# Swapping weights and stream in the output matmuls of a chunked linear attention ahead of two expert layers

## The chip, the cores and the metric

The kernel runs on one core of a Trainium2 chip. The metric is the device time of one launch, in microseconds. Two per cent of it is 22 us.

## The reference

A gated linear attention feeds a top-2 mixture of experts, and that a dense two-layer network. There are 4 batches, 8 heads, 768 steps, head dimension 48; so 3072 tokens of 384 features.

```python
for t in range(S):
    state = alpha[:, :, t, :, None] * state + k[:, :, t, :, None] * v[:, :, t, None, :]
    y[:, :, t] = einsum('bhd,bhde->bhe', q[:, :, t], state)
x = y as tokens x (heads * 48)
noisy = x @ w_gate + log1p(exp(x @ w_noise)) * noise      # 8 experts
top 2 of noisy, softmax of the two -> weights
x = sum over the two experts of weight * (relu(x @ w1[e]) @ w2[e])   # F = 1024
h = x @ w_in                                               # 2048
return max(0.01 * h, h) @ w_out
```

## The kernel before

**Attention** works on 24 units: a unit is 128 consecutive tokens of one batch, all eight heads, two heads of a pair side by side on the partitions (rows 0 to 47 and 64 to 111). Four units make a tile (six tiles), six units a batch. Per unit, by the names of the code: SyncE loads `at` (decays), `kq` (keys and queries), `nv` (values, tokens on rows); VectorE scans the decays (`back`, `forth`) and scales keys and queries (`keys` L918, `queries` L922); TensorE transposes the keys (`turn_k` L930), makes the scores of each head (`score` L943, 48 rows of one half of the array for each head of a pair), ScalarE copies them out of the accumulator, GpSimd masks them in two halves (`mask_s` L952, tile `am`). The state goes on through `update` L975 and `carry` L979, GpSimd decays it (`sp`, L968).

The output of a unit collects in the accumulator tile `pY`, tokens on rows. `within` (L996) adds masked scores times values: the weights are 128 columns of `am`, the stream 48 columns of `nv`, four matmuls for the even heads and four for the odd ones in two steps. `across` (L1001) adds queries times decayed state: the weights are the queries `qp` of a pair, the stream 96 columns of `sp`; the first unit of a batch has none. `copy_y` (L1017) copies `pY` into the tile's `x`, and SyncE stores it to `x_d` in DRAM (L1022).

**Routing** per tile: `turn_x` (L1040) transposes the four units' `x` in twelve pieces, `copy_x` (L1045) copies them, `logits` (L1050) multiplies them by the gate weights in three matmuls of 512 columns, `turn_back` (L1059) brings tokens back on rows; VectorE picks the top two, and GpSimd scatters token numbers into slots by indirect DMA (L1148).

**Experts** (`gemm1` L668, `gemm2` L707) run on rows gathered from `x_d` (L510, transposed at L528), weights split in two parts for three matmuls each; the dense network follows with the same lines. The first two experts' groups need the routing and the stores of the first four tiles only; their slot numbers come in by one DMA (`load_idx` L505).

All instructions are put in order by a list scheduler, `Planner`: each step has an engine, a duration, what it depends on, buffer rings that it takes, and a due time; `plan.run(1, core)` writes out the attention stage, `plan.run(2)` the rest. Every engine, SyncE's queue of DMAs too, then runs its list strictly in that order. Matmuls are plain fp32 in attention and routing; each leaves two records in the profile.

A second function, `general`, holds a slower way for inputs outside certain bounds; it stands in a branch that these inputs don't take.

Of the kernel before, what the change touches and what calls it, by code (L numbers as in the profile page):

```python
# [323 lines left out]
def tile_kernel(  # L324
# [16 lines left out]
    wgn_l: bass.AP,  # L341
    noise_l: bass.AP,
# [53 lines left out]
    wgn = consts.tile([128, KD, 2 * E], FT)  # L396
# [433 lines left out]
    with ExitStack() as actx:  # L830
# [13 lines left out]
            at=5, kq=4, nv=5, suf=3, wt=3, kt=4, qp=4, pM=2, kN=2, pS=1, pT=1, ar=2, am=2, sp=2, S=2, pY=1, x=2, xt=1,  # L844
# [7 lines left out]
        def build_unit(u):  # L852
# [118 lines left out]
            if not last:  # L971
                def update():
                    d["pu"] = psum.tile([PP, HP, P2], FT, name="pM", bufs=2)
                    for p in range(HP):
                        nc.tensor.matmul(d["pu"][:, p, :], d["kN"][:, p, :], d["v"][:, p * P2:(p + 1) * P2],  # L975
                                         start=p == 0, stop=first, skip_group_check=True)
# [9 lines left out]
                up = add("p", 0.72, update, use=[(ck, R["kN"]), (LV, R["nv"])], takes=[R["pM"]], due=b + 3.2)  # L986
# [16 lines left out]

            w0 = add("p", 0.92, lambda: within(0), use=[(sel[0], R["am"]), (LV, R["nv"])], takes=[R["pY"]],
                     due=b + PERIOD + 3)
            w1_ = add("p", 0.92, lambda: within(1), [w0, sel[1]], use=[(sel[0], R["am"]), (LV, R["nv"]), (w0, R["pY"])],
                      due=b + PERIOD + 4)
            done = w1_
            if not first:
                done = add("p", 0.92, across, [w1_], use=[(qq, R["qp"]), (dc, R["sp"]), (w0, R["pY"])],  # L1010
                           due=b + PERIOD + 5)
# [7 lines left out]
            cy = add("a", 0.5, copy_y, [done] + xs[T], use=[(w0, R["pY"])] + ([(xs[T][0], R["x"])] if c else []),  # L1019
                     takes=[] if c else [R["x"]])  # L1020
            xs[T].append(cy)
            xo = add("s", 0.07, lambda: nc.sync.dma_start(x_d[u * C:(u + 1) * C, :], X[T][:, c, :]), [cy],  # L1022
                     use=[(xs[T][0], R["x"])], size=0.2)
# [7 lines left out]
        def build_turn(T, gr, keep):  # L1031
# [3 lines left out]
            def turn_x(d):  # L1035
                if d == 0 and T == gr[0]:
                    keep["lg"] = rt.tile([128, NG * len(gr), 2 * E], FT, name="lg")
                k["px", d] = ps2.tile([128, TT], FT, name="pA")
# [3 lines left out]
            def copy_x(d):  # L1042
                if d == 0:
                    k["xt"] = early.tile([128, KD, TT], FT, name="xt", bufs=1)
                nc.scalar.activation(k["xt"][:, d, :], k["px", d], AF.Copy)  # L1045

            def logits():
                k["pl"] = ps2.tile([2 * E, TT], FT, name="pA")
                for d in range(KD):
                    nc.tensor.matmul(k["pl"], wgn[:, d, :], k["xt"][:, d, :], start=(d == 0), stop=(d == KD - 1))  # L1050

            def copy_l():
                k["lt"] = k["xt"][:2 * E, 0, :]
                nc.scalar.activation(k["lt"], k["pl"], AF.Copy)

            def turn_back():
                k["pb"] = ps2.tile([128, NG, 2 * E], FT, name="pA")
                for c in range(NG):
                    nc.tensor.transpose(k["pb"][:, c, :], k["lt"][:, c * C:(c + 1) * C], identf[:2 * E, :2 * E])  # L1059

            def copy_back():
                nc.scalar.activation(keep["lg"][:, n0:n0 + NG, :], k["pb"], AF.Copy)

            b = at_unit(4 * T + 5)
            cp = []
            before = done_of.get(("chain", RGROUPS.index(gr) - 2), [])[-1:]
            for d in range(KD):
                tx = add("p", 0.46, lambda d=d: turn_x(d), xs[T] + before, use=[(xs[T][0], R["x"])], takes=[R["pA"]],
                         due=b + 2 + 2 * d)
                core.append(tx)  # L1070
                cp.append(add("a", 0.61, lambda d=d: copy_x(d), use=[(tx, R["pA"])] + ([(cp[0], R["xt"])] if d else []),
                              takes=[] if d else [R["xt"]]))
# [361 lines left out]
```

## Time and profile before

| | us |
|---|---|
| median of 3 runs | 1101.55 |
| lowest and highest run | 1100.0, 1129.27 |
| profiled execution, its own time | 1096.46 |
| span of its trace | 1094.7 |

The span runs from the first to the last instruction of the profiled execution; 1.8 us of its own time lie around it. The median of the runs is 5.1 us above the profiled execution's time. Attention and routing take about the first 195 us of the span, the experts and the dense network the rest.

### The profile page before, as it was taken

Reading aid. Unit: us, or ns where it says so; the run is one execution under the profiler, and the core shown is the slowest. Engines: PE = TensorE matmul, PEld = TensorE weight load, DVE = VectorE, ACT = ScalarE, POOL = GpSimd, SP = SyncE. Lnnn points to the kernel's source line nnn. Section 1 sums busy time; section 2 is a strip of 40 time slices with the busy share of each in tenths; the row PEclk is TensorE's granted clock in tenths of the full one; section 3 lists DMA queues with packets and bytes.
Section 4 is the critical chain, followed back from the end, with each engine's and each line's share of the span. In section 5 each row is a group of like instructions: output and inputs, shape, how many; then the busy total and the mean of one; then the engine's idle time right before and its main releaser. Section 6 shows DMA issues by size and latency. Waiting matters only on the chain.

```text
span 1094.7 us, 17345 instructions
## 1 busy us (share of the span) xinstructions
PE 1068.6 (98%) x6404; PEld 1017.5 (93%) x6404; DVE 586.8 (54%) x1199; ACT 389.1 (36%) x829; POOL 324.6 (30%) x386
## 2 busy tenths in 40 slices
PE   7999998999999999999999999999999999999997
PEld 6877886899999999999999999999999999999997
DVE  8588974522445554754565334554555555454543
ACT  3665553322344453533453333231222212121211
POOL 3457766531113333444253131320111102010000
PEclk9999896999999999999999999999999999999999
DMA  9868832233345364655566555320101111100000
GB/s 245 239 180 194 176 82 86 39 92 107 121 124 184 125 208 148 209 168 154 172 206 226 198 190 181 115 66 7 59 12 55 29 37 30 37 23 22 1 23 25
DMA packets 76965, 125.76 MB, mean 115 GB/s; under 512 B 10407, under 2 KB 57383, under 8 KB 76871
## 3 DMA queue, kind: packets, MB, share of 16 engines
q1 hardware_dynamic: 68679, 104.47, 31.9%
q0 software_dynamic: 8192, 20.09, 6.5%
q8 instruction: 52, 0.85, 0.3%
q14 instruction: 42, 0.34, 0.1%
HBM read 91.84 MB, written 32.69 MB: 114 GB/s over the span
## 4 chain that ended last, share of the span: by engine, by line
PE 93%; POOL 2%; issue 2%; DVE 1%; ACT 1%; DMA 1%; POOLq 0%; ACTq 0%; DVEq 0%
PE py L707 40%; PE ph L668 39%; PE pY L996 3%; PE pA L528 2%; PE pS L943 2%; PE pY L1001 2%; PE pM L975 1%; PE pA L1050 1%; PE pM L979 1%; DMA at<-in_al_l_dram 1%; PE pM L930 1%; PE pA L1040 1%; POOL am L952 1%; POOL idx_d L1148 1%; DVE kt L918 0%
## 5 line engine op out<-in xcount | busy, mean ns | idle before, releaser
L692 DVE SCALAR_TENSOR_TENSOR hl<-ph,hh 128x384 fp32r<-128x384 f32 (+1 forms) x128 | 77.6, 606 | 202.7 <-ACT hh L685 186.6
L678 ACT ACTIVATE hc<-ph 128x384 f32<-128x384 f32 x128 | 62.9, 492 | 294.9 <-PE ph L668 289.6
L681 DVE SCALAR_TENSOR_TENSOR hc<-hc 128x384 f32<-128x384 f32 x128 | 71.5, 558 | 174.6 <-ACT hc L678 173.0
L685 ACT ACTIVATE hh<-ph 128x384 fp32r<-128x384 f32 (+1 forms) x128 | 68.0, 531 | 261.3 <-PE ph L668 247.8
L707 PE MATMUL py<-w2hA,hh 128*128 128x384 f32 (+1 forms) x416 | 142.1, 342 | 0.0
L707 PE MATMUL py<-w2hB,hh 128*128 128x384 f32 (+1 forms) x416 | 141.7, 341 | 0.0
L707 PE MATMUL py<-w2hA,hl 128*128 128x384 f32 (+1 forms) x416 | 140.5, 338 | 0.0
L707 PE MATMUL py<-w2lA,hh 128*128 128x384 f32 (+1 forms) x416 | 140.2, 337 | 0.0
L707 PE MATMUL py<-w2lB,hh 128*128 128x384 f32 (+1 forms) x416 | 140.0, 337 | 0.0
L707 PE MATMUL py<-w2hB,hl 128*128 128x384 f32 (+1 forms) x416 | 140.0, 337 | 0.0
L668 PE MATMUL ph<-xh,w1hA 128*128 128x384 f32 (+1 forms) x384 | 136.0, 354 | 0.9 <-issue 0.9
L668 PE MATMUL ph<-xl,w1hA 128*128 128x384 f32 (+1 forms) x384 | 134.2, 350 | 0.2 <-issue 0.2
L668 PE MATMUL ph<-xh,w1hB 128*128 128x384 f32 (+1 forms) x384 | 133.9, 349 | 0.0
L668 PE MATMUL ph<-xh,w1lA 128*128 128x384 f32 (+1 forms) x384 | 133.9, 349 | 0.0
L668 PE MATMUL ph<-xl,w1hB 128*128 128x384 f32 (+1 forms) x384 | 133.6, 348 | 0.0
L668 PE MATMUL ph<-xh,w1lB 128*128 128x384 f32 (+1 forms) x384 | 133.5, 348 | 0.0
L730 POOL DMA_INDIRECT xg<-y_d,gidx x48 | 48.7, 1015 | 263.2 <-PE pA L528 212.5
L510 POOL DMA_INDIRECT xg<-x_d,idx x56 | 55.7, 994 | 106.4 <-PE pA L528 87.0
L707 PEld LDWEIGHTS py<-w2hA,hh 128*128 128x128 f32 (+1 forms) x416 | 77.3, 186 | 1.2 <-issue 0.3
L707 PEld LDWEIGHTS py<-w2lA,hh 128*128 128x128 f32 (+1 forms) x416 | 77.3, 186 | 0.9
L707 PEld LDWEIGHTS py<-w2lB,hh 128*128 128x128 f32 (+1 forms) x416 | 77.3, 186 | 1.0
L707 PEld LDWEIGHTS py<-w2hB,hh 128*128 128x128 f32 (+1 forms) x416 | 77.3, 186 | 0.8
(153 smaller groups left out, 1989.0 us busy)
## 6 DMA issues: line engine op xcount, KB each, us to landing
w1s<-in_moe_w_dram SPq DMA_DIRECT2D x32, 384.0 KB
w2s<-in_moe_w_dram SPq DMA_DIRECT2D x32, 384.0 KB
kq<-in_kq_l_dram SPq DMA_DIRECT2D x24, 448.0 KB
w1s<-in_moe_w_in_dram SPq DMA_DIRECT2D x24, 256.0 KB
w2s<-in_moe_w_out_dram SPq DMA_DIRECT2D x16, 384.0 KB
y_d<-ys SPq DMA_DIRECT2D x32, 180.0 KB
at<-in_al_l_dram SPq DMA_DIRECT2D x24, 226.2 KB
nv<-in_v_l_dram SPq DMA_DIRECT2D x24, 192.0 KB
```

What stands on the lines that cost most here:

```text
L510: nc.gpsimd.indirect_dma_start(out=xg[:n, :], out_offset=None, in_=x_d[0:rows, :], in_offset=bass.IndirectOffsetOnAxis(ap=idx_sb[i][:n, j, ...
L528: nc.tensor.transpose(p[:, d, :n], src[:n, d * 128:(d + 1) * 128], identf[:n, :n])
L668: nc.tensor.matmul(ps[:, :n], a[:, d, fo:fo + 128], x[:, d, :n], start=i == 0, stop=i == len(seq) - 1)
L678: nc.scalar.activation(hc[:, :n], ps[:, :n], AF.Copy)
L681: nc.vector.scalar_tensor_tensor(hc[:, :n], hc[:, :n], 0.01, hc[:, :n], op0=OP.mult, op1=OP.max)
L685: nc.scalar.activation(hh[:, :n], ps[:, :n], AF.Relu)
L692: nc.vector.scalar_tensor_tensor(hl[:, :n], ps[:, :n], 0.0, hh[:, :n].bitcast(FT), op0=OP.max, op1=OP.subtract)
L707: nc.tensor.matmul(py[:n, :], h[:, o:o + n], w[:, f % 2, :], start=(f == 0 and i == 0), stop=(f == nf - 1 and i == 2))
L730: nc.gpsimd.indirect_dma_start(out=yg, out_offset=None, in_=y_d[0:rows, :], in_offset=bass.IndirectOffsetOnAxis(ap=gidx[:, c, kk:kk + 1], ...
L943: nc.tensor.matmul(d["pa", i][:, p], d["kt"][r, p], d["qp"][r, p], start=True, stop=True)
L996: nc.tensor.matmul(d["py"][:, p, i * D:(i + 1) * D], d["am"][:, i, p, :], d["v"][:, h * D:(h + 1) * D], start=h == 0, stop=first, skip_gro ...
L1001: nc.tensor.matmul(d["py"][:, p, :], d["qp"][:, p], d["sp"][:, p].rearrange("p s d -> p (s d)"), start=False, stop=True, skip_group_check= ...
```

## The change

`within` now uses 64 columns of values as weights (48 and 16 zeros) and streams the 128 columns of masked scores; the even head of a pair writes rows 0 to 63 of `pY`, the odd one rows 64 to 127. `across` uses 48 columns of the state as weights and streams the queries, into the same halves. So `pY` has features on rows, tokens on columns. It is copied as it is into the tile's `xt`; `logits` reads it from there, in four matmuls for the four head pairs, with gate weights that are laid out the same way with zeros between (`wgp_l`). For the store to `x_d`, each unit's output is transposed by four matmuls (`turn_y`) and copied once more (`copy_x`). The values are padded on the host to 64 columns a head, and `update` reads its 96 columns in two pieces of 48. `turn_x` and its copies are gone. `within` is one step that needs both halves of the mask. Due times and durations in the planner follow. Line numbers after the diff are 1 higher from L339 on, and differ by a few more behind L996.

```diff
-    wgn = consts.tile([128, KD, 2 * E], FT)
+    wgn = consts.tile([128, HP, 2 * E], FT)
...
-            at=5, kq=4, nv=5, suf=3, wt=3, kt=4, qp=4, pM=2, kN=2, pS=1, pT=1, ar=2, am=2, sp=2, S=2, pY=1, x=2, xt=1,
+            at=5, kq=4, nv=5, suf=3, wt=3, kt=4, qp=4, pM=2, kN=2, pS=1, pT=1, ar=2, am=2, sp=2, S=2, pY=1, x=3, xt=2, lt=1,
...
-                d["v"] = loads.tile([128, Dm], FT, name="nv", bufs=5)
-                nc.sync.dma_start(d["v"], v_l[u * C:(u + 1) * C, :])
+                d["v"] = loads.tile([128, H, 64], FT, name="nv", bufs=5)
+                nc.sync.dma_start(d["v"].rearrange("p h d -> p (h d)"), v_l[u * C:(u + 1) * C, :])
...
-                        nc.tensor.matmul(d["pu"][:, p, :], d["kN"][:, p, :], d["v"][:, p * P2:(p + 1) * P2],
+                        nc.tensor.matmul(d["pu"][:, p, :], d["kN"][:, p, :], d["v"][:, 2 * p:2 * p + 2, 0:D],
...
-            def within(i):
-                if i == 0:
-                    d["py"] = psum.tile([128, HP, P2], FT, name="pY", bufs=1)
+            def within():
+
+                d["py"] = psum.tile([128, HP, C], FT, name="pY", bufs=1)
                 for p in range(HP):
-                    h = 2 * p + i
-                    nc.tensor.matmul(d["py"][:, p, i * D:(i + 1) * D], d["am"][:, i, p, :], d["v"][:, h * D:(h + 1) * D],
-                                     start=h == 0, stop=first, skip_group_check=True)
+                    for i in range(2):
+                        nc.tensor.matmul(d["py"][64 * i:64 * i + 64, p], d["v"][:, 2 * p + i, :], d["am"][:, i, p, :],
+                                         start=p == 0, stop=first, skip_group_check=True)
...
-                    nc.tensor.matmul(d["py"][:, p, :], d["qp"][:, p], d["sp"][:, p].rearrange("p s d -> p (s d)"),
-                                     start=False, stop=True, skip_group_check=True)
...
+                    for i in range(2):
+                        nc.tensor.matmul(d["py"][64 * i:64 * i + D, p], d["sp"][:, p, i, :], d["qp"][:, p],
+                                         start=False, stop=True, skip_group_check=True)
+
+            w0 = add("p", 1.0, within, use=[(s_, R["am"]) for s_ in sel[:1]] + [(LV, R["nv"])], deps=sel, takes=[R["pY"]],
+                     due=b + PERIOD + 4)
...
-                    X[T] = work.tile([128, NG, Dm], FT, name="x")
-                nc.scalar.activation(X[T][:, c, :], d["py"].rearrange("p h d -> p (h d)"), AF.Copy)
...
+                    X[T] = work.tile([128, NG, HP, C], FT, name="xt")
+                nc.scalar.activation(X[T][:, c], d["py"], AF.Copy)
+
+            def turn_y():
+                d["px"] = ps2.tile([128, HP, C], FT, name="pA")
+                for p in range(HP):
+                    nc.tensor.transpose(d["px"][:, p, :], X[T][:, c, p, :], identf)
+
+            def copy_x():
+                d["x"] = work.tile([128, HP, 2, D], FT, name="x", bufs=3)
+                nc.scalar.activation(d["x"], d["px"].rearrange("p h (s d) -> p h s d", s=2)[:, :, :, 0:D], AF.Copy)
...
+            ty = add("p", 0.46, turn_y, [cy], use=[(xs[T][0], R["xt"])], takes=[R["pA"]], due=b + PERIOD + 8)
+            cx = add("a", 0.5, copy_x, use=[(ty, R["pA"])], takes=[R["x"]])
+            xo = add("s", 0.07, lambda: nc.sync.dma_start(x_d[u * C:(u + 1) * C, :], d["x"].rearrange("p h s d -> p (h s d)")),
+                     use=[(cx, R["x"])], size=0.2)
...
-                for c in range(NG):
-                    nc.tensor.transpose(k["px", d][:, c * C:(c + 1) * C], X[T][:, c, d * 128:(d + 1) * 128], identf)
...
-                nc.scalar.activation(k["xt"][:, d, :], k["px", d], AF.Copy)
...
-                k["pl"] = ps2.tile([2 * E, TT], FT, name="pA")
-                for d in range(KD):
-                    nc.tensor.matmul(k["pl"], wgn[:, d, :], k["xt"][:, d, :], start=(d == 0), stop=(d == KD - 1))
...
+                k["pl"] = ps2.tile([2 * E, NG, C], FT, name="pA")
+                for p in range(HP):
+                    nc.tensor.matmul(k["pl"], wgn[:, p, :], X[T][:, :, p, :], start=(p == 0), stop=(p == HP - 1))
```

How the instructions of TensorE move, first around the logits of the first tile. `pA` is the accumulator of transposes and logits, `xg` the gathered rows, `ph` and `py` the experts' accumulators. Before:

```order
L943 MATMUL pS<-qp,kt 128x128 x8
L979 MATMUL pM<-sp,identf 112x384
L1040 MATMUL pA<-identf,x 128x128 x8
L996 MATMUL pY<-nv,am 128x48 x4
L1040 MATMUL pA<-identf,x 128x128 x4
L996 MATMUL pY<-nv,am 128x48 x4
L943 MATMUL pS<-qp,kt 128x128 x8
L1050 MATMUL pA<-xt,wgn 16x512 x3
L1001 MATMUL pY<-sp,qp 128x96 x4
L930 MATMUL pM<-identf,kt 128x112 x4
L1059 MATMUL pA<-identf,xt 128x16 x4
```

With the change:

```order
L997 MATMUL pY<-am,nv 64x128 x8
L1022 MATMUL pA<-identf,xt 128x128 x4
L1003 MATMUL pY<-qp,sp 48x128 x8
L944 MATMUL pS<-qp,kt 128x128 x8
L980 MATMUL pM<-sp,identf 112x384
L1050 MATMUL pA<-xt,wgn 16x512 x4
L1022 MATMUL pA<-identf,xt 128x128 x4
L931 MATMUL pM<-identf,kt 128x112 x4
L944 MATMUL pS<-qp,kt 128x128 x8
L1059 MATMUL pA<-identf,lt 128x16 x4
```

The twelve transposes of a tile (x8 and x4) ahead of the logits are gone; transposes x4 of single units stand between the other groups, one of them behind the logits; `within` is x8 in one place and has 64-column weights, `across` is x8.

The end of the attention stage on TensorE, up to the first transposes of gathered rows. Before:

```order
L1001 MATMUL pY<-sp,qp 128x96 x4
L1119 LDWEIGHTS tri
L1119 MATMUL pA<-ot,tri 128x32
L1120 LDWEIGHTS ones_b
L1120 MATMUL pA<-acc,ones_b 128x32
L996 MATMUL pY<-nv,am 128x48 x8
L1001 MATMUL pY<-sp,qp 128x96 x4
L1040 MATMUL pA<-identf,x 128x128 x12
L528 MATMUL pA<-identf,xg 128x128 x3
L1050 MATMUL pA<-xt,wgn 16x512 x3
L528 MATMUL pA<-identf,xg 128x128 x3
L1059 MATMUL pA<-identf,xt 128x16 x4
```

With the change:

```order
L1022 MATMUL pA<-identf,xt 128x128 x8
L997 MATMUL pY<-am,nv 64x128 x8
L1022 MATMUL pA<-identf,xt 128x128 x4
L1003 MATMUL pY<-qp,sp 48x128 x8
L1050 MATMUL pA<-xt,wgn 16x512 x4
L1113 LDWEIGHTS tri
L1113 MATMUL pA<-ot,tri 128x32
L1114 LDWEIGHTS ones_b
L1114 MATMUL pA<-acc,ones_b 128x32
L1022 MATMUL pA<-identf,xt 128x128 x4
L1059 MATMUL pA<-identf,lt 128x16 x4
L529 MATMUL pA<-identf,xg 128x128 x12
```

The last logits stand ahead of the position matmuls (`tri`) of the tile before, the transposes of gathered rows behind all of attention and not between its last groups.

SyncE's queue at the same place, `x_d<-x` being the stores of the output and `idx` the slot numbers of the first experts. Before:

```order
L1022 DMA x_d<-x 128x384
L870 DMA nv<-in_v_l_dram 128x384
L1022 DMA x_d<-x 128x384
L866 DMA kq<-in_kq_l_dram 112x1024
L1022 DMA x_d<-x 128x384 x4
L505 DMA idx_119<-idx_d 128x24
L1022 DMA x_d<-x 128x384
```

With the change:

```order
L1033 DMA x_d<-x 128x384
L871 DMA nv<-in_v_l_dram 128x512
L867 DMA kq<-in_kq_l_dram 112x1024
L1033 DMA x_d<-x 128x384 x9
L506 DMA idx_119<-idx_d 128x24
L1033 DMA x_d<-x 128x384
L444 DMA w1s<-in_moe_w_dram 128x3x256 x2
L447 DMA w2s<-in_moe_w_dram 128x2x384 x2
```

The slot numbers are loaded behind 23 of the 24 stores in both; nine stores stand together ahead of them where there were four.

## Rows read from the trace of the kernel before

**Rows 1.** Page, part 1: busy time, share of the span, instructions.
```profile
PE 1068.6 (98%) x6404; PEld 1017.5 (93%) x6404; DVE 586.8 (54%) x1199; ACT 389.1 (36%) x829; POOL 324.6 (30%) x386
```

**Rows 2.** Page, part 4: the chain that ended last, by line.
```profile
PE py L707 40%; PE ph L668 39%; PE pY L996 3%; PE pA L528 2%; PE pS L943 2%; PE pY L1001 2%; PE pM L975 1%; PE pA L1050 1%; PE pM L979 1%; DMA at<-in_al_l_dram 1%; PE pM L930 1%; PE pA L1040 1%; POOL am L952 1%; POOL idx_d L1148 1%; DVE kt L918 0%
```

**Rows 3.** Stretches: length, busy us (x instructions) of each engine, granted clock, DMA share, GB/s.
```profile
23.20:112.00 88.80, 84.64 (x750) 71.08 (x751) 69.19 (x155) 52.81 (x124) 53.30 (x79) 1.00 0.81 212
112.00:118.70 6.70, 6.70 (x38) 5.81 (x35) 6.36 (x15) 3.74 (x10) 5.40 (x8) 0.50 0.63 126
118.70:170.00 51.30, 48.75 (x412) 39.45 (x411) 41.98 (x105) 27.28 (x66) 35.09 (x52) 1.00 0.48 109
170.00:187.00 17.00, 15.53 (x77) 14.02 (x77) 3.58 (x19) 5.16 (x11) 8.12 (x9) 0.50 0.23 67
...
193.80:197.30 3.50, 3.28 (x10) 2.80 (x11) 3.36 (x11) 1.98 (x4) 2.63 (x3) 0.51 0.69 58
197.30:1091.00 893.70, 889.53 (x5026) 869.10 (x5024) 437.30 (x859) 283.58 (x587) 205.98 (x201) 1.00 0.33 103
```

**Rows 4.** Waits of TensorE, 0 to 165 us: total us, times, longest.
```profile
PE pY L996 <- POOL am L952: 2.7, 4, 1.2
```

**Rows 5.** Timeline, 11 to 181 us: start us, us, engine, line, tiles, count [idle before <-releaser].
```profile
11.81 1.94 PE L996 MATMUL pY<-nv,am 128*128 128x48 f32 x8 [0.23 <-POOL am L952]
...
168.21 2.05 DVE L918 TENSOR_TENSOR kt<-kq,suf 112x512 f32<-112x512 f32 x1
...
170.31 1.01 PE L930 MATMUL pM<-identf,kt 112*128 112x112 f32 x4 [1.64 <-DVE kt L918]
...
177.51 3.62 PE L996 MATMUL pY<-nv,am 128*128 128x48 f32 x16 [0.57 <-POOL am L952]
```

**Rows 6.** Timeline, 87 to 90 us: one within group, loads and matmuls.
```profile
87.78 1.86 PEld L996 LDWEIGHTS pY<-nv,am 128*128 128x128 f32 x16 [1.69 <-POOL am L952]
...
87.80 1.96 PE L996 MATMUL pY<-nv,am 128*128 128x48 f32 x16 [1.09 <-POOL am L952]
```

**Rows 7.** Timeline of TensorE, 34 to 40 us.
```profile
34.27 1.00 PE L996 MATMUL pY<-nv,am 128*128 128x48 f32 x8
35.20 1.16 PE L943 MATMUL pS<-qp,kt 48*128 48x128 f32 x16
36.29 1.09 PE L996 MATMUL pY<-nv,am 128*128 128x48 f32 x8
37.22 0.99 PE L975 MATMUL pM<-nv,kN 128*112 128x96 f32 x8
38.05 1.06 PE L1001 MATMUL pY<-sp,qp 112*128 112x96 f32 x8
39.03 1.16 PE L943 MATMUL pS<-qp,kt 48*128 48x128 f32 x16
```

**Rows 8.** Timeline of TensorE, 62 to 71 us: transposes and logits.
```profile
62.92 1.09 PE L1040 MATMUL pA<-identf,x 128*128 128x128 f32 x8
63.85 0.94 PE L975 MATMUL pM<-nv,kN 128*112 128x96 f32 x8
...
65.28 0.60 PE L1040 MATMUL pA<-identf,x 128*128 128x128 f32 x4
65.72 0.99 PE L996 MATMUL pY<-nv,am 128*128 128x48 f32 x8
...
67.73 2.75 PE L1050 MATMUL pA<-xt,wgn 128*16 128x512 f32 x6
70.41 1.09 PE L996 MATMUL pY<-nv,am 128*128 128x48 f32 x8
```

**Rows 9.** Groups by line, ScalarE, 23 to 168 us: the copies.
```profile
L1017 ACT ACTIVATE x<-pY 128x384 f32<-128x384 f32 x21 | 10.3, 489 | 14.4 <-PE pY L1001 9.2 <-issue 1.4 <-PE pY L996 1.4
...
L1045 ACT ACTIVATE xt<-pA 128x512 f32<-128x512 f32 x15 | 8.8, 598 | 0.9 <-PE pA L1040 0.7
```

**Rows 10.** Page, part 6: loads of the values, KB each.
```profile
nv<-in_v_l_dram SPq DMA_DIRECT2D x24, 192.0 KB
```

More of the change, by code (lines that the diff above doesn't have):

```diff
@@ L341, in tile_kernel @@
     wgn_l: bass.AP,
+    wgp_l: bass.AP,
     noise_l: bass.AP,
@@ L984, in step @@
                     nc.scalar.activation(d["S"], d["pu"].rearrange("p h (s d) -> p h s d", s=2), AF.Copy)
-                up = add("p", 0.72, update, use=[(ck, R["kN"]), (LV, R["nv"])], takes=[R["pM"]], due=b + 3.2)
+                up = add("p", 0.9, update, use=[(ck, R["kN"]), (LV, R["nv"])], takes=[R["pM"]], due=b + 3.2)
                 if not first:
@@ L1033, in build_turn @@
             k = {}
[L1035 to L1038, printed above, removed]
-                for c in range(NG):
-                    nc.tensor.transpose(k["px", d][:, c * C:(c + 1) * C], X[T][:, c, d * 128:(d + 1) * 128], identf)
-            def copy_x(d):
-                if d == 0:
-                    k["xt"] = early.tile([128, KD, TT], FT, name="xt", bufs=1)
-                nc.scalar.activation(k["xt"][:, d, :], k["px", d], AF.Copy)
             def logits():
-                k["pl"] = ps2.tile([2 * E, TT], FT, name="pA")
-                for d in range(KD):
-                    nc.tensor.matmul(k["pl"], wgn[:, d, :], k["xt"][:, d, :], start=(d == 0), stop=(d == KD - 1))
+                keep["lg"] = rt.tile([128, NG, 2 * E], FT, name="lg")
+                k["pl"] = ps2.tile([2 * E, NG, C], FT, name="pA")
+                for p in range(HP):
+                    nc.tensor.matmul(k["pl"], wgn[:, p, :], X[T][:, :, p, :], start=(p == 0), stop=(p == HP - 1))
             def copy_l():
-                k["lt"] = k["xt"][:2 * E, 0, :]
+                k["lt"] = early.tile([2 * E, NG, C], FT, name="lt", bufs=1)
                 nc.scalar.activation(k["lt"], k["pl"], AF.Copy)
@@ L1058, in turn_back @@
                 for c in range(NG):
-                    nc.tensor.transpose(k["pb"][:, c, :], k["lt"][:, c * C:(c + 1) * C], identf[:2 * E, :2 * E])
+                    nc.tensor.transpose(k["pb"][:, c, :], k["lt"][:, c], identf[:2 * E, :2 * E])
             def copy_back():
-                nc.scalar.activation(keep["lg"][:, n0:n0 + NG, :], k["pb"], AF.Copy)
+                nc.scalar.activation(keep["lg"][:, n0:n0 + NG, :], k["pb"][:, :, 0:2 * E], AF.Copy)
             b = at_unit(4 * T + 5)
-            cp = []
             before = done_of.get(("chain", RGROUPS.index(gr) - 2), [])[-1:]
[L1067 to L1072, printed above, removed]
-            lg = add("p", 1.35, logits, [consts_in] + cp, use=[(cp[0], R["xt"])], takes=[R["pA"]], due=b + 8)
-            cl = add("a", 0.6, copy_l, [lg], use=[(lg, R["pA"]), (cp[0], R["xt"])])
-            tb = add("p", 0.35, turn_back, [cl], use=[(cp[0], R["xt"])], takes=[R["pA"]], due=b + 10)
+            lg = add("p", 3.4, logits, [consts_in] + xs[T] + before, use=[(xs[T][0], R["xt"])], takes=[R["pA"]], due=b + 3)
+            core.append(lg)
+            cl = add("a", 0.6, copy_l, use=[(lg, R["pA"])], takes=[R["lt"]])
+            tb = add("p", 0.45, turn_back, use=[(cl, R["lt"])], takes=[R["pA"]], due=b + 5)
             return add("a", 0.25, copy_back, [tb], use=[(tb, R["pA"])])
@@ L1217, in tile_kernel, with general @@
     with tc.If(fv > 0):
-        general(tc, dict(q=q, k=k, v=v, alpha=alpha), identf, hm, desc, wgn, noise, x_d, w1, w2, w_in, w_out, out)
-def general(tc, src, identf, hm, desc, wgn, noise, x_d, w1, w2, w_in, w_out, out):
+        general(tc, dict(q=q, k=k, v=v, alpha=alpha), identf, hm, desc, wgn_l, noise, x_d, w1, w2, w_in, w_out, out)
+def general(tc, src, identf, hm, desc, wgn_l, noise, x_d, w1, w2, w_in, w_out, out):
     nc = tc.nc
@@ L1276, in general @@
         TG = NG * 128
+        wgn = gw.tile([128, KD, 2 * E], FT, name="hwg")
+        nc.sync.dma_start(wgn, wgn_l)
         with tc.For_i(0, N // TG, 1) as it:
@@ L1401, in _laid_out @@
         "kq_l": _np.ascontiguousarray(kq.reshape(kq.shape[0], 64 + d, -1)),
-        "v_l": _np.ascontiguousarray(inputs["v"].transpose(0, 2, 1, 3)).reshape(b * s, h * d),
+        "v_l": _np.pad(inputs["v"].transpose(0, 2, 1, 3), ((0, 0), (0, 0), (0, 0), (0, 64 - d))).reshape(b * s, h * 64),
         "wgn_l": _np.ascontiguousarray(wgn.reshape(-1, 128, 2 * e).transpose(1, 0, 2)),
+        "wgp_l": _np.ascontiguousarray(wgp.reshape(h // 2, 128, -1).transpose(1, 0, 2)),
         "noise_l": _np.ascontiguousarray(inputs["moe_noise"].reshape(n // 128, 128, e).transpose(1, 0, 2)),
```

17 lines of the change are left out of this document (6 added, 11 removed).

## Prediction

> **What bounds the kernel now.** I read the page's first part first: TensorE is busy 98% of the span, VectorE 54% and the rest less [rows 1]. The chain of waits says the same: nearly all of it is TensorE lines, 79% of it the two expert lines, which the change does not touch [rows 2]. Then the table by stretches [rows 3]: everything the diff edits lies ahead of about 195 us; the 894 us behind it are expert work and stay as they are. Up to 170 us TensorE is busy 95% of each long stretch, so the attention stage is bound by what TensorE issues, not by a wait: the one repeated wait in it, for the mask from GpSimd, adds up to 2.7 us [rows 4]. VectorE comes second: 78% of the stretch up to 112 us, 82% of the one up to 170 us. Last, two stretches in the stage, and a short one after it, have a granted clock of about 0.5: 112.0 to 118.7, 170.0 to 187.0, 193.8 to 197.3, together 27.2 us. There the same 16 within records take 3.62 us [rows 5] instead of 1.96 [rows 6]. Before 23 us, where that column reads 1.00, the records run as slowly: a group of x8 at 11.81 takes 1.94 us [rows 5].
>
> So the question is how much TensorE time one chunk of 128 tokens needs before and after. I take it from the timeline of TensorE, always from the start of a group to the start of the next, since durations overlap [rows 7, 8].
>
> **The change part by part.** Every fp32 matmul leaves two records, so 8 matmuls are "x16".
>
> Within (masked scores by values): before, 8 matmuls per chunk in two groups of x8, each with a 128-column weight load of masked scores and 48 columns of values streamed. 34.27 to 35.20 and 36.29 to 37.22 are 0.93 us each [rows 7], so 1.86 us per chunk. After, 8 matmuls whose weights are 64 columns of values and whose stream is 128 columns, alternately into the lower and upper 64 output rows. No row of before shows two column halves at work together. The near row is the scores line: also 8 matmuls, 128 columns streamed, alternately on two halves, there of the rows. It takes 35.20 to 36.29 = 1.09 us [rows 7]. That two of them run at once is seen against the logits row: 6 records of 512 columns take 2.68 us (67.73 to 70.41) [rows 8], which is 0.112 us per 128 columns; 16 such records one by one would need 1.79 us. Eight pairs need 0.90; the other 0.19 us of the 1.09 I count as the price of going into and out of halves. Bounds for the new group: 0.90 us and 1.79 us plus 0.19. I take 1.09, the row of the same shape. Saving 0.77 us a chunk, 24 chunks: -18.5 us.
>
> The Trainium skill speaks against this in TensorE: Matmul & The Clock Gate, Part 3 (the mechanism): a weight load overlaps a running matmul only when the row group differs, and column halves share their rows. The rows here show otherwise for full-width weights: the 16 loads of a within group cover 1.86 us of the 1.96 us in which its 16 matmuls run [rows 6]. By the rule, an estimate from the same rows: half a load is 0.058 us, a pair then costs two of them and 0.112, a group 1.8 us, and the sum below would turn from -8 to some +23 us.
>
> Across (queries by state): before 4 matmuls, 38.05 to 39.03 = 0.98 us [rows 7]; after 8 with 48-column weights and 128 columns streamed, in the same halves. By the scores row 1.09: +0.11 on the 20 chunks that have it, +2.2 us (bounds as above, 0.90 to 1.98).
>
> Transposes of the output: before 12 per tile of four chunks, 0.93 us for eight and 0.44 for four [rows 8], 1.37 together; after four per chunk, 16 per tile, 1.83. Six tiles: +2.8 us.
>
> Logits: before 3 matmuls of 512 columns, 2.68 us [rows 8]; after 4, since each of four head pairs has 128 rows with padding: 3.57 us. Six tiles: +5.4 us.
>
> Update streams the same 96 columns in two pieces of 48 with a gap. It is bound by its weight loads (0.83 us for 8 records, 37.22 to 38.05), so I take 0; bounds 0 and +0.1 us a chunk. Carry and keys' transposes are untouched.
>
> Sum on TensorE: -18.5 + 2.2 + 2.8 + 5.4 = -8.1 us at full clock. About a quarter of the chunks' work ran at half speed (before 23 us, and in the low stretches), where the same saving counts double: -2.0.
>
> Other engines. ScalarE: copies of 512 columns instead of 384 out of the accumulator (0.598 against 0.489 us [rows 9]), one more copy per chunk (0.489), less three of 0.598 per tile: 24 x 0.11 + 24 x 0.49 - 18 x 0.60 = +3.6 us over a stage in which it is busy 59% at most [rows 3]; hidden. It would cost those 3.6 us if ScalarE became the last to arrive. Values grow from 192 to 256 KB a chunk [rows 10], 1.57 MB in all, 7 us of transfer at the 212 GB/s of the stretch up to 112 us; loads run up to five chunks ahead, so hidden; without that cover up to +7.
>
> Waits. Within used to start with the first mask; now it needs both, and behind it in TensorE's queue stand across, scores and the transposes of other chunks. The accumulator pY has one buffer, so the next within also waits for the copy of this one, now 0.11 us longer. Bounds: 0, and the longest such wait of before, 1.2 us [rows 4], on each of 24 chunks, 29. Most withins stand behind other groups of TensorE, as they did, so I take +2, near the 2.7 of all these waits before.
>
> Clock. At 170 us a wait of 1.64 us for VectorE stands ahead of the fall to half speed [rows 5]; the change does not touch what was waited for. Bounds of what the new, denser groups do: all 27.2 us of low clock gone, -13.6; or one more stretch of 17 us, +8.5. I take the first short stretch, which has no such wait ahead of it, as gone and no more: -3.4.
>
> Total -8.1 - 2.0 + 2.0 - 3.4 = -11.5 us: 1085 against the profiled execution's own 1096.5. The runs shown have a median of 1101.55, 5 us above it, so I say 1090.
>
> At the stage's end little moves. The load of the first experts' indices still stands behind all but one of the 24 stores of x in SyncE's queue, and these now need a transpose and a copy more (about 1 us); but logits no longer wait for twelve transposes and three copies.
>
> **The rivals.** 1. The column halves don't run together. For it: no row of before shows them. Against it: row halves do. (The rule of the Trainium skill above would end near the same time.) Price: 16 x 0.112 + 0.19 = 1.98 us instead of 1.09, +0.89 on 24 + 20 groups = +39 as the far end; without the 0.19 (nothing to switch between) +0.70 x 44 = +31. Against -8.1 that is +23 to +31: about 1127, slower. It decides as soon as a pair needs more than about 0.135 us (0.18 us more per group eats the 8).
>
> 2. Another engine takes the bound: after 112 us VectorE is at 82%, and GpSimd at 68%, with their records stretched when both run (the keys' product at 168.21 takes 2.05 us [rows 5]). Then TensorE's saving comes out as waits: 0 +- 4, about 1100. Against it: TensorE needs some 6% less, and 82% becomes only 87%.
>
> 3. The clock stays up: within no longer leaves TensorE loading weights most of the time, and all three low stretches go: -8.1 - 13.6 = -21.7, about 1080. Against it: the wait for VectorE at 168 us and the wait for the gathered rows at 187 to 194 us remain.
>
> **How the numbers follow.** Forecast 0.52 (1083 to 1097); rival 1 0.08 (1115 to 1135); rival 2 0.20 (1096 to 1106); rival 3 0.20 (1072 to 1083). Two per cent is 22 us, about what a measurement of this kernel can tell from no change. Below 1079.5 lies the better part of rival 3: 0.14. Above 1123.6 most of rival 1: 0.06. The range 1074 to 1108 leaves out rival 1 and the edges of 2 and 3.
>
> **What would show it.** Within as x16 in about 1.1 us from start to start, and across the same; if either is near 1.8, rival 1 holds. Logits x8 near 3.6 us. TensorE's waits up to 165 us below 8 us after its first matmul, or rival 2 holds, and then the waits name VectorE or GpSimd. Low-clock stretches in the attention stage fewer than 27 us. The steady expert work begins some 12 us before 197.3. An expert stage that changes in length by more than 2 us would make the forecast wrong in its premise.

## The result, and the profile after it

The changed kernel takes 1091.23 us (median of 4 runs, 1090.0 to 1092.44) against 1102.22 us for the kernel before run beside it: a ratio of 0.991, with a 95% interval of 0.9885 to 0.9934. The ratio leaves out the one slow run of the kernel before, at 1129.27 us. That is a gain of about 1%, "same" by the 2% bound, and 1.2 us from the forecast of 1090. It is not the whole result. The same kernel was run twice more, beside the experiments, on two different chips: 1102.67 us at a ratio of 0.9937 (0.9898 to 0.9975), and 1101.79 us at 1.0001 (0.9974 to 1.0029). All three lie in the forecast's range and in its middle class, but the last is no gain at all. Single runs of the kernel before lie between 1091 and 1129 us, those of the changed kernel within 6 us of one another each time it was run, so a ratio to the kernel before is less firm than the changed kernel's own time. So there are two questions: whether the steps of the sum were right, and why one program takes 1091 us here and 1102 there.

First the profile of the first run. Part 1 of the page; [rows 1] has the same line of before:

```profile
PE 1056.3 (97%) x6600; PEld 989.9 (91%) x6600; DVE 585.1 (54%) x1199; ACT 392.2 (36%) x835; POOL 325.3 (30%) x386
```

TensorE's busy time fell by 12.3 us. Its timeline from 24 to 38 us (start, duration, engine, line, operation, tiles, count; L997 is within, L1003 across, L1022 the transposes of the output, L944 the scores, L976 the update, L1050 the logits), against [rows 7] and [rows 8]:

```profile
24.52 1.09 PE L997 MATMUL pY<-am,nv 128*64 128x128 f32 x16
25.55 0.90 PE L980 MATMUL pM<-sp,identf 112*112 112x384 f32 x2
26.38 1.08 PE L1003 MATMUL pY<-qp,sp 112*48 112x128 f32 x16
27.39 0.66 PE L1022 MATMUL pA<-identf,xt 128*128 128x128 f32 x4
27.88 0.94 PE L976 MATMUL pM<-nv,kN 128*112 128x96 f32 x8
28.75 1.09 PE L997 MATMUL pY<-am,nv 128*64 128x128 f32 x16
...
33.29 3.61 PE L1050 MATMUL pA<-xt,wgn 128*16 128x512 f32 x8
36.83 0.66 PE L1022 MATMUL pA<-identf,xt 128*128 128x128 f32 x4
```

From start to start, within takes 24.52 to 25.55 = 1.03 us for a whole chunk, where before two groups of 0.93 did it; across takes 1.01, four transposes 0.49, the update 0.87, the logits 3.54. The two column halves run together: record by record, the products of a pair start 0.007 us apart (24.684 and 24.691), and the next pair 0.11 us later.

The stretches of the first run (length, busy time and count of PE, PEld, DVE, ACT and POOL, granted clock, DMA share, GB/s), against [rows 3]:

```profile
80.60:90.80 10.20, 8.81 (x59) 6.49 (x60) 9.79 (x21) 4.45 (x9) 7.32 (x12) 0.50 1.10 194
...
121.50:124.90 3.40, 3.40 (x32) 3.07 (x32) 3.30 (x10) 0.65 (x2) 1.03 (x4) 0.50 0.83 53
...
183.00:193.20 10.20, 6.20 (x22) 5.08 (x22) 8.22 (x19) 7.09 (x15) 8.07 (x8) 0.50 0.74 227
193.20:1088.60 895.40, 888.79 (x5024) 868.67 (x5022) 438.15 (x862) 284.49 (x588) 208.34 (x203) 1.00 0.33 103
```

The reader is to see the three lines of stretches at half clock (0.50, the 1.2 GHz level): 10.2 + 3.4 + 10.2 = 23.8 us, against 27.2 before. The last across starts at 172.91 us, 8.0 us earlier than the 180.93 of before; the steady expert work starts at 193.2, only 4.1 earlier, so half of the gain is given back between the stages. The expert work from there to the end is 2.0 us shorter (895.4 against 1094.7 - 197.3 = 897.4).

TensorE's waits from 7.8 to 165 us (total, times, longest; the kt line holds the 7.5 us ahead of the first matmul, and three lines of 0.3 us and less are left out), against [rows 4]:

```profile
PE pM L931 <- DVE kt L919: 7.7, 2, 7.5
PE pY L997 <- POOL am L953: 5.3, 2, 3.9
PE pM L980 <- POOL sp L969: 2.4, 2, 1.7
PE pY L997 <- POOL tots L902: 0.8, 1, 0.8
PE pM L976 <- ACT kN L935: 0.6, 1, 0.6
```

The mask (am) is now waited for twice, once for 3.9 us, and the falls of the clock at 80.6 and 121.5 us stand right behind such waits, for the mask up to 80.18 us and for sp up to 120.18:

```profile
80.18 0.43 PE L997 MATMUL pY<-am,nv 128*64 128x128 f32 x2 [3.92 <-POOL am L953]
...
120.18 0.90 PE L980 MATMUL pM<-sp,identf 112*112 112x384 f32 x2 [1.74 <-POOL sp L969]
...
172.91 1.08 PE L1003 MATMUL pY<-qp,sp 112*48 112x128 f32 x16
```

The third line is the last across. GpSimd's timeline tells why the mask is late: it issues seven scatters of the router's choices in a row, most of them 1.28 us apart, ahead of it.

```profile
70.39 1.20 POOL L1142 DMA_INDIRECT idx_d<-tok,si  x1 [0.68 <-DVE wt L898]
...
78.31 1.16 POOL L1142 DMA_INDIRECT idx_d<-tok,si  x1 [0.30 <-issue]
79.47 0.66 POOL L953 TENSOR_SCALAR_AFFINE_SELECT am<-ar 128x512 f32<-128x512 f32 x1
```

In the kernel before the scatters of these tiles stood between the masks, one to four in a row; with the change's new dependences the planner places those of each of the first three tiles in runs of seven or eight.

### The profile page after: what moved, and what is told of

The parts are those of the page before. It is cut to its first block, busy times and chain, and to the rows that moved or that the text cites. A ratio compares the mean times of both kernels' runs of the same rounds, so it can differ in the third digit from the quotient of the medians.

```text
span 1088.6 us, 17738 instructions
## 1 busy us (share of the span) xinstructions
PE 1056.3 (97%) x6600; PEld 989.9 (91%) x6600; DVE 585.1 (54%) x1199; ACT 392.2 (36%) x835; POOL 325.3 (30%) x386
## 4 chain that ended last, share of the span: by engine, by line
PE 82%; issue 0%; DVE 0%; ACT 0%; DMA 0%; ACTq 0%
PE py L708 40%; PE ph L669 39%; PE pA L529 2%; DVE w1lB L457 0%; ACT ys L718 0%; DVE w2lB L457 0%; ACT w1hB L453 0%; DVE xl L538 0%; PE pA L557 0%; DVE g_um L201 0%; DVE g_u L193 0%; DMA x_d<-x 0%; ACTq L453 0%; PE pA L1113 0%; ACTq L718 0%
```

## The experiments

The kernels ran in four series, each series on one chip with its own runs of the kernel before. The expectations of the first series (experiments 1 to 3) took 1091 us as the time of the changed kernel, which did not run in that series; experiment 4 showed that comparisons have to stay within a series.

**1. Are the halves worth what the sum says?** Within alone, then within and across, issue the products of the lower half first and then those of the upper, instead of alternately; nothing else moves.

```diff
-                for p in range(HP):
-                    for i in range(2):
+                for i in range(2):
+                    for p in range(HP):
```

> The changed kernel, but within takes all four even heads (lower output half) and then all four odd ones (upper half), so neighbours in TensorE's queue use the same column half; the order of all else is the same. Theory A (the saving comes from two column halves working at once): each within group goes from 1.03 us to 16 x 0.112 = 1.8 us from start to start, +0.77 x 24 = +18 us, total about 1110. Theory B (it comes from the smaller weight load and the longer stream alone, halves or not): the group stays near 1.03 us, total 1091 +- 3.

> As the run before, with across ordered by halves too. Theory A: across also goes from 1.01 to about 1.8 us on 20 chunks, another +15 us, total about 1125, which is slower than the kernel before the change. Theory B: 1091 +- 3.

Measured: 1110.09 us (ratio 1.0094, 1.0058 to 1.0129) and 1117.37 us (1.0147, 1.0085 to 1.0209). The first total is what the theory of the halves asked for, and its reason is still not the right one, as the timeline of the second kernel shows:

```profile
25.39 1.58 PE L997 MATMUL pY<-am,nv 128*64 128x128 f32 x16
26.90 0.90 PE L980 MATMUL pM<-sp,identf 112*112 112x384 f32 x2
27.73 1.55 PE L1003 MATMUL pY<-qp,sp 112*48 112x128 f32 x16
29.21 0.66 PE L1022 MATMUL pA<-identf,xt 128*128 128x128 f32 x4
```

A group takes 1.51 us (25.39 to 26.90) and across 1.48, not the 1.8 expected: record by record, the upper half's first starts at 25.88 us, behind five of the lower's eight records, and from there the two run together, so the halves still overlap in part. That is 0.48 us on 24 groups, 11.5 us; the other part of the 19 us against 1091 had to come from elsewhere. Between these two kernels, on one chip, the 20 across groups alone differ: (1.48 - 1.01) x 20 = 9.4 us expected from the rows, 7.3 measured, with 3.4 us less at half clock in the second's profile.

**2. Are the runs of scatters what costs the waits?** The scatters of the first three tiles are held in pairs behind the masks of successive chunks.

```diff
+        behind = {}
...
+            for s_ in behind.get(u, []):
+                s_.deps.append(sel[1])
...
+            if gr[0] < EARLY_TILES - 1:
+                for n_, s_ in enumerate(sc):
+                    behind.setdefault(5 * gr[0] + 9 + n_ // 2, []).append(s_)
```

> The changed kernel, with the eight scatters of each of the first three tiles held in pairs behind the masks of successive chunks, instead of seven or eight in a row in GpSimd's queue. Theory C (the runs of scatters are where a part of TensorE's saving is given back): the waits for the mask at 76 to 84 us (5.3 us) go, and the low-clock stretch of 10.2 us behind them with it (5.1 us): 6 to 10 us off, total 1081 to 1085. Rival D (VectorE or the end of the stage would take over): waits of the same size appear elsewhere, total 1091 +- 3.

Measured: 1088.68 us (0.9907, 0.9872 to 0.9942), 2.5 us under the first run of the changed kernel. Held against that run theory C missed, and rival D held: 1088.68 lies in its 1091 +- 3, and its profile has 6.1 us of waits for the keys (kt), where those for the mask are down to 1.7. But the changed kernel did not run in this series; experiment 5 has the two on one chip, and there it looks otherwise.

**3. Is the give-back between the stages the late last store?** In the changed kernel the logits of the last tile stand ahead of the last chunk's transposes, so the last store of x is late. The chain of the changed kernel there (start, us):

```profile
180.23 0.09 DMA x_d<-x
180.32 3.19 issue
...
183.60 0.85 ACT w1hB L453
```

ScalarE stands 3.2 us in front of a weight copy (L453) that waits for this store, and the copy of the first gathered rows stands behind it. The edit makes the last tile's logits depend on the last chunk's transposes.

```diff
-            lg = add("p", 3.4, logits, [consts_in] + xs[T] + before, use=[(xs[T][0], R["xt"])], takes=[R["pA"]], due=b + 3)
+            lg = add("p", 3.4, logits, [consts_in] + xs[T] + before + ([st[NCH - 1]["ty"]] if T == NT - 1 else []), use=[(xs[T][0], R["xt"])], takes=[R["pA"]], due=b + 3)
```

> The changed kernel, with the last chunk's transpose (and so its copy and store) ahead of the last logits. Theory E (the store of the last chunk holds ScalarE for 3.3 us at 180 us, and with it the first expert's rows): the first expert matmul moves from 189.4 to about 186, total 1087 to 1088. Rival F (the gathered rows come last anyway): total 1091 +- 1.

Measured: 1107.31 us (1.0069, 1.0041 to 1.0096), which neither theory named: 16 us over the first run of the changed kernel, though all engines have the same order up to some 175 us. Its trace lay behind that of the changed kernel from 76 us on, long before the edit. So something other than the edit differed.

**4. The same kernel again.** The second series runs the changed kernel once more, the two edits of 2 and 3 together, and the spread kernel with products not alternating.

> The changed kernel once more, beside the two that follow. Theory S (TensorE's completions are held back during runs of scatters only in some programs, and the same program behaves the same each time): 1091 within 2 us, and in its profile no matmul whose semaphore arrives over 0.6 us after its recorded end, as in the first profile of it. Rival (the holding back is chance from one execution to the next): late semaphores here too, by some 20 to 30 us in all, and a time 5 to 15 us higher.

> The scatters of the first three tiles spread in pairs, and the last tile's logits behind the last chunk's transposes, both at once. Theory S (the 16 us that the moved logits alone cost came from TensorE's completions arriving 3 to 7 us late in the runs of scatters, not from the move itself): with the runs broken the loss is gone, 1083 to 1090, and the transition gains the 3.3 us that ScalarE waits for the last store of x before its first weight copy. Rival (the moved logits cost by themselves, by the order at the end of the stage): the spread kernel's 1088.7 plus about 16, 1101 to 1107.

> The spread kernel with within's eight products issued as four for the lower half and then four for the upper. In the profile of the same edit without the spread a group took 1.51 us from its first matmul to the next group's (26.18 to 27.69) where alternating took 1.03, so 0.48 us on 24 groups = 11.5 us at full clock, some 13 with the part at half clock. Theory A1 (the halves are worth those 13 us, and the other 6 of that edit's 19 us were late completions in the runs of scatters): 1088.7 + 13 = 1102 within 3. Theory A (all 19 us are the halves): 1107 or more. Rival (the order within a group costs nothing where TensorE waits anyway): under 1094.

Measured: the changed kernel again 1102.67 us (0.9937). A late signal here is one whose recorded event comes over half a us behind the recorded end of its product, with ScalarE idle until that event; there are six in its attention stage, the latest by 6.7 us, 24 us in all. So the theory that one program always behaves alike fell, and with it every comparison with 1091. Spread and turn together: 1095.58 us (0.9862, 0.9771 to 0.9953), between what theory S and its rival named, and 7 us below the changed kernel of its series. The third kernel's edit was meant for within and, as two loops read alike, fell on the scores; its expectation speaks of within and is not tested by it, for what ran has the scores' products not alternating and within as it was. It took 1109.06 us (0.9991, 0.9951 to 1.0031), and its timeline gives the price of the row halves:

```profile
28.91 1.71 PE L945 MATMUL pS<-qp,kt 48*128 48x128 f32 x16
30.55 1.09 PE L1000 MATMUL pY<-am,nv 128*64 128x128 f32 x16
```

Scores need 1.64 us (28.91 to 30.55) where alternating they need 1.09. Row halves and column halves answer alike to the order of issue.

**5. All on one chip.** The third series holds the changed kernel, experiment 1's first edit, the spread kernel, and spread with turn against one another.

> The changed kernel, as the base of the three that follow on the same chip: 0.991 to 0.994 of the time before. It has been seen at 1091 and at 1103 us on two chips, so the others are to be held against this run and not against 1091.

> Within's eight products as four lower and then four upper, all else as in the changed kernel. Theory A1 (0.48 us on each of 24 groups, 11.5 us, some 13 with the part at half clock): 13 above the changed kernel of this call, within 3. Theory A (the 19 us found across calls are all the halves): 18 or more above it. Rival (TensorE waits for masks anyway): under 5 above it.

> The scatters in pairs. Theory S (what the spreading takes away are TensorE's late completions in the runs of scatters): where the changed kernel's profile of this call shows over 20 us of late semaphores, 8 to 14 us below it; where it shows none, 0 to 4 below. Theory D (the runs of scatters cost only the waits for the mask, which the keys' waits take over): 0 to 4 below it in either case.

> The spread kernel and the last logits behind the last transposes. Theory T (ScalarE's first weight copy then no longer waits 3.3 us for the last store of x, and the first gathered rows' copy behind it comes earlier): 1 to 5 us below the spread kernel of this call. Rival (the logits later hold up the last tile's routing, and the first experts' positions with it): 3 or more above the spread kernel.

Measured, in this order: 1101.79 (1.0001, 0.9974 to 1.0029), 1109.03 (1.0076, 1.005 to 1.0101), 1088.87 (0.9891, 0.9845 to 0.9937), 1095.12 us (0.9965, 0.9931 to 0.9999). The changed kernel's ratio is above the 0.991 to 0.994 that was expected. Each kernel had nearly the same time as in the earlier series, the changed kernel too (1102.67 there); only its first run, 1091, stands alone.

The changed kernel of this series, first TensorE from 72 to 83 us, then ScalarE:

```profile
72.11 1.08 PE L1003 MATMUL pY<-qp,sp 112*48 112x128 f32 x16
...
74.88 0.72 PE L1059 MATMUL pA<-identf,lt 16*128 16x16 f32 x4
77.12 1.08 PE L1022 MATMUL pA<-identf,xt 128*128 128x128 f32 x4 [1.52 <-issue]
82.19 1.11 PE L1022 MATMUL pA<-identf,xt 128*128 128x128 f32 x4 [4.00 <-ACT lg L1062]
```

```profile
76.09 0.60 ACT L1017 ACTIVATE xt<-pY 128x512 f32<-128x512 f32 x1 [3.96 <-PE pA L1059]
...
77.52 0.54 ACT L935 ACTIVATE kN<-pM 128x448 f32<-128x448 f32 x1 [0.46 <-remote]
81.92 0.22 ACT L1062 ACTIVATE lg<-pA 128x64 f32<-128x64 f32 x1 [3.85 <-remote]
```

L1017 copies what across (L1003) left, done by 73.19, and starts at 76.09; L1062 copies the logits' transposes (L1059), done by 75.60, and starts at 81.92. ScalarE was idle both times. In the first run, with the same order on both engines and the scatters at the same times, these two started at 73.31 and 75.28:

```profile
73.31 0.60 ACT L1017 ACTIVATE xt<-pY 128x512 f32<-128x512 f32 x1 [1.11 <-PE pY L1003]
...
75.28 0.22 ACT L1062 ACTIVATE lg<-pA 128x64 f32<-128x64 f32 x1 [0.55 <-PE pA L1059]
```

So TensorE's results were there and the signal that they were came 3 to 6 us late. The same is seen at 114 to 121 us and at 153 us, always in a run of GpSimd's scatters. TensorE has the same order in both runs, and only at these three places does the later run fall behind: by 3, 6 and 12 us in all. In these runs of scatters TensorE's own records pause too, once between the two records of a single carry:

```profile
118.84 0.58 PE L980 MATMUL pM<-sp,identf 112*112 112x384 f32 x1
119.84 0.56 PE L980 MATMUL pM<-sp,identf 112*112 112x384 f32 x1 [0.42 <-issue]
```

In the first run these two take 0.90 us together, and the trace names nothing that the second waited for here. TensorE also waits for ScalarE's late copies, and the clock falls. Its longest waits from 7.8 to 165 us, and its stretches at half clock:

```profile
PE pM L931 <- ACT S L985: 4.3, 1, 4.3
PE pA L1022 <- ACT lg L1062: 4.0, 1, 4.0
PE pM L976 <- ACT kN L935: 2.4, 1, 2.4
PE pA L1022 <- issue: 1.5, 1, 1.5
```

```profile
77.20:94.30 17.10, 11.64 (x74) 8.56 (x76) 11.35 (x32) 7.36 (x17) 10.27 (x15) 0.50 0.85 163
...
121.60:128.40 6.80, 4.46 (x18) 3.60 (x18) 6.66 (x16) 3.38 (x8) 4.24 (x9) 0.50 0.35 90
...
155.70:165.90 10.20, 8.25 (x48) 6.32 (x49) 6.75 (x20) 4.52 (x10) 4.44 (x8) 0.50 0.05 16
...
193.20:203.50 10.30, 5.20 (x17) 3.81 (x18) 6.79 (x15) 5.96 (x13) 8.47 (x7) 0.50 0.78 231
```

That is 44.4 us at half clock against 23.8 in the first run, but TensorE waits for a good part of it, so the price is not half of the difference. Up to the last across, which starts at 185.21 us where the first run has 172.91, TensorE's waits come to 16.7 us against 10.1, and it works 24.4 us at half clock (11.64 + 4.46 + 8.25) against 12.2, half of which is time lost: 6.6 + 6.1 = 12.7, near the 12.3 us between the two starts. The medians differ by 10.6.

The spread kernel of this series has two such stretches, with a wait of 5.6 us for the keys' product in the first:

```profile
88.60:95.40 6.80, 4.58 (x36) 4.01 (x36) 6.59 (x13) 1.76 (x4) 2.41 (x4) 0.50 0.99 237
...
180.80:194.40 13.60, 7.99 (x28) 6.78 (x29) 9.46 (x23) 8.20 (x17) 10.55 (x11) 0.50 0.65 201
```

That is 20.4 us in all, 24.0 less than the changed kernel of its series. Its last across starts at 170.83 us, 14.4 earlier than there; 5.3 of that is given back before the steady expert work, which starts at 194.4 (against 203.5). The two spans differ by 8.9 us and the medians by 12.9, as the profiled execution of the spread kernel, 1092.86 us, is the slowest of its six. In its attention stage TensorE's signals were late by at most 1.9 us, and the time is what theory S forecast: the long delays stand in the runs of scatters, and breaking these up is worth 13 us where the delays are. What it is worth without them is not shown: 1088.68 against the first run's 1091.23 compares two series, and by the ratios, 0.9907 and 0.991, nothing is left.

Experiment 1's edit costs 7.2 us here. By the rows it is 0.49 us on 24 groups, 11.8, less 1.6 us of waits and 1.3 for 2.6 us less of TensorE's work at half clock: 8.9, near the difference of the two spans, 1108.4 - 1100.0 = 8.4. Theory A1 named 13 within 3: it had the group right and the waits and the clock not.

Spread with turn is 6.2 us slower than spread, so theory T fell and its rival held. TensorE's timeline between the stages shows where:

```profile
174.12 4.71 PE L1054 MATMUL pA<-xt,wgn 128*16 128x512 f32 x8
...
182.65 0.42 PE L1063 MATMUL pA<-identf,lt 16*128 16x16 f32 x4 [3.66 <-ACT lt L1058]
187.31 0.90 PE L529 MATMUL pA<-identf,xg 128*128 128x128 f32 x3 [4.24 <-DMA xg<-x_d,idx]
```

and without the edit:

```profile
182.22 0.88 PE L529 MATMUL pA<-identf,xg 128*128 128x128 f32 x3 [3.62 <-DMA xg<-x_d,idx]
```

The logits come later and run at half clock, and the first gathered rows reach TensorE at 187.31 us instead of 182.22. ScalarE's first weight copy does start earlier, at 179.00 us instead of 180.81; but four of these copies now stand ahead of the copy of the logits (L1058), which starts at 182.03 instead of 176.96. That costs more than the earlier start saves.

**6. Is the gain the spread's own?** The edit of experiment 2, in the kernel before.

> The kernel before, with the scatters of its first three tiles in pairs as in the spread kernel. Theory Q (the kernel before already has them in short groups between the masks, and its profile shows only 3 us of late semaphores in the attention stage, so there is little to take away; what the spread kernel has over the kernel before, 12 to 13 us, is then the change's own worth): ratio 0.996 to 1.003. Theory P (the spreading is worth the same 12 to 13 us to either kernel, and the change by itself nothing): ratio 0.986 to 0.990.

Measured: 1114.39 us (1.0097, 1.0062 to 1.0131), slower, so neither theory named it. In this kernel the spread does not pay, so what the spread kernel has over the kernel before is not the spread's own: it takes both edits together. A wait and a long stretch at half clock are in its profile too:

```profile
83.40 0.57 PE L931 MATMUL pM<-identf,kt 112*128 112x112 f32 x4 [1.61 <-DVE kt L919]
```

```profile
84.10:111.40 27.30, 26.67 (x139) 23.31 (x138) 16.75 (x41) 11.73 (x24) 13.88 (x17) 0.50 0.78 146
```

One wait of 1.61 us for the keys' product, at 81.8 to 83.4 us, stands ahead of 27.3 us at half clock, the longest seen. There are no late signals in its profile.

The spread kernel took 1088.68 and 1088.87 us on two chips, ratios 0.9907 and 0.9891 to the kernel before. It beats the changed kernel in the one series that ran both; the changed kernel's first run, at 0.991, is level with it.

## Why the prediction came out as it did

**Within, -18.5: right, a little small.** The group takes 1.03 us, not 1.09, so 24 x 0.83 = -19.9. The Trainium skill's rule in TensorE: Matmul & The Clock Gate, Part 3 (the mechanism), by which a weight load overlaps a running matmul only where the row group differs, does not hold for these column halves: by it a group would take about 1.8 us, and the trace has 1.03. Even with the halves not alternating it is 1.51. Rival 1, that the halves don't run together, fell with that.

**Across, +2.2: too much.** 1.01 us against 0.98, so 20 x 0.03 = +0.6.

**Transposes +2.8 and update 0: somewhat too little. Logits +5.4: right.** Four transposes take 0.49 to 0.59 us start to start, 1.96 to 2.36 a tile against 1.37, so +3.5 to +5.9 on six tiles, 4.7 in the middle; logits 3.54 against 2.68, +5.2; the update 0.87 against 0.83, +0.8 on 20 chunks. The sum at full clock becomes -19.9 + 0.6 + 4.7 + 5.2 + 0.8 = -8.6 us, where the prediction had -8.1.

**Half-clock work, -2.0: a gain was missed.** TensorE's records run at full speed from about 15.7 us instead of 23.2 (the clock column reads 1.00 in both). Within at 13.10 still takes 1.91 us, at half speed; the transposes at 16.41 run at full. 7.5 us less at half clock is worth some 3.7 us, and no step named it.

**Waits, +2: the term that was mis-sized.** The prediction looked for "below 8 us" of TensorE's waits after the first matmul; the first run has 10.1, and 5.3 of it is the mask behind GpSimd's scatters. The kernel before has 5.6 in the same window (2.7 for the mask [rows 4], 1.2 ahead of other within groups, 1.7 in pieces of 0.5 and less), so the term measured +4.5 and not +2. In the third series it is 16.7 us, 10.7 of it in three waits for ScalarE, which waits for late signals. The prediction looked at what stands behind within in TensorE's queue, and not at what the change does to GpSimd's order, where runs of seven and eight scatters stand in place of one to four.

**Clock, -3.4 (bounds -13.6 to +8.5): right in the first run, not in the repeats.** Counted as the prediction counts, by half of the length, 23.8 us at half clock instead of 27.2 give -1.7. Counted by half of TensorE's work in these stretches, 18.4 us instead of 25.5, it is -3.6. The stretch at 112 us, which it took as gone, has no counterpart there, but two others came, at 80.6 and 121.5. In the repeat 44.4 us give +8.6 by length, the bound worked out as "one more stretch of 17 us", and +2.0 by the work in them, 29.6 us; the rest is waits.

**"At the stage's end little moves": wrong by 4 us.** From the start of the last across to the steady expert work it was 16.4 us before and is 20.3 now, with ScalarE's 3.2 us for the last store of x in it. The step weighed the later stores against the freed logits and left out that the first weight copy waits for the last of them.

**Values' DMA and ScalarE's 3.6 us, hidden: nothing shown against it.** Neither appears among the waits above. **Experts unchanged within 2 us:** 2.0 by the clock's rise, at the edge of what was asked.

So 1090 was met in the first run by a sum that was right in its work terms, with misses on either side: about 3.7 us more from the early clock, against some 2.5 us more of waits than allowed for and 4 at the stage's end. By the two profiled spans, 1094.7 and 1088.6, the change is -6.1 us: -8.0 up to the last across, +3.9 between the stages, -2.0 in the experts. The forecast of the profiled execution was 1085, and it took 1090.42, 5.4 us more. The median was forecast 5 us above the profiled execution, as in the runs of the kernel before; the changed kernel's median lies 0.8 above. So by medians the change is -11.0 us, near the -11.5 of the sum, for the most part because the runs of the kernel before lie far apart. In the repeats rival 2, that the saving comes out as waits (about 1100, 0.20), describes the time, but by another mechanism: not VectorE or GpSimd at their limit, but signals that come late while GpSimd scatters, and half clock behind them. The range held both levels; that the likeliest case met the first of them to 1.2 us was luck.

What stays open is why the first run of the changed kernel had no late signal, at the same times of its scatters, and two others had them in the same places. The profiles hold one sign. In those two, semaphore events are missing from the record, and not of TensorE alone: in the third series 783 of TensorE's are there for 810 matmuls that send one, 756 of ScalarE's for 811 instructions and 1114 of VectorE's for 1175, where the first run's profile has all of them. Of the fourteen profiles only that one and the one of experiment 6 are complete, and only these two have no late signal; the twelve others, those of the kernel before and of the spread kernel among them, miss some and have some late. So late signals go with gaps in the record. That the recording itself holds TensorE back is a rival that no run here tests, and another is what differs between the chips. What was shown is that in the series with late signals the long ones stand in the runs of scatters, and that breaking the runs up gave 1089 us in both series where it was tried alone. Whether it gives anything where the record is complete was not run.

## What to carry to other kernels

Price a change in matmul shape by the nearest group of the same shape, from start to start, and issue products for two halves of the array alternately: here that was worth 0.5 us a group (1.03 against 1.51). Then read what the new dependences do to the order on every other engine, here GpSimd with its scatters above all, for a wait of a few microseconds on TensorE can cost itself and then half of the work in a low-clock stretch behind it. Before a difference of 1% is believed, run the changed kernel again beside its variants on another chip, and look whether the profiles to be compared are equally complete.

## What the runs showed of the hardware that was not expected

Column halves of the array, with separate weights and separate streams, run together as row halves do: 1.03 us for eight products of 128 columns against 1.09 for row halves. Issued half after half they still overlap in part, 1.51 and 1.64 us.

In the third series TensorE's semaphore reached ScalarE 3 to 6 us after the recorded end of the matmul, with ScalarE idle, while GpSimd issued indirect scatters 1.28 us apart. What waited for ScalarE in the same stretches started within 0.1 us of its recorded end: VectorE at 82.44 us, for instance, 0.04 us behind it. Delays of this kind are seen only in profiles with gaps in their record.

Of the falls of the granted clock whose stretches are shown here, each lies in or right behind a wait of TensorE of 1.1 to 5.6 us, but for two in the kernel before, at 111.9 and 193.8 us, with no wait over 0.8 us in the 5 us ahead of them. The stretch at half speed that followed was between 3.4 and 27.3 us long, with TensorE busy for 26.7 us of the longest one.
